# Moving most of a transpose stage, at the hand-over between two layers, into the turns of the loop before it

## The chip, the cores and the metric

The kernel runs on one core of a Trainium2 chip. The metric is the device time of one execution in microseconds (us); lower is better.

Engines are written as in the profile: PE is the matrix engine, PEld its weight loads, DVE is VectorE, ACT is ScalarE, POOL is GpSimd, SP issues DMAs. "L1211" is line 1211 of that kernel's source. The same statement has another line number in another kernel; a table below gives the ones that matter.

## The reference, cut to what matters

Four layers follow each other, A, B, A, B, each with a layer norm in front and a residual sum behind. `x` has 2048 tokens of width 640, in bf16.

```python
def _A_ref(x, w_r, w_i):                       # a 2D Fourier filter
    X = rfft2(x.astype(float32), axes=(-2, -1))
    X = X * (w_r + 1j * w_i)
    return irfft2(X, s=(S, D), axes=(-2, -1)).astype(bfloat16)

def _B_ref(x, mem0, Wq, Wk, Wv, Wo, seg_len):  # attention over 64 segments of 32 tokens
    mem = mem0
    for s in range(n_seg):
        h = concatenate([mem, x[:, s*seg_len:(s+1)*seg_len, :]], axis=1)
        # ... q, k, v, masked softmax, output projection o ...
        mem = o[:, :M, :].copy()
        outs.append(o[:, M:, :])

x = x + _A_ref(_layernorm(x), A_w_r, A_w_i)
x = x + _B_ref(_layernorm(x), B_mem0, B_Wq, B_Wk, B_Wv, B_Wo, B_seg_len)
x = x + _A_ref(...)                            # the same two layers once more
x = x + _B_ref(...)
```

The change touches the hand-over from A to B, which occurs twice (the prediction calls the two "layer 1" and "layer 2"). Layer A ends with an inverse DFT that yields `x` in 16 row tiles of 128 tokens. Layer B needs the normed `x` transposed (width on the partitions) in a buffer `hT`, and the sum of each segment, `u`, for a first guess of the memory.

## The kernel before: the parts that matter

The last stage of layer A. One turn computes one half transform (`psg`), evicts it on ACT, computes one row tile (`psy`), evicts it on ACT, and takes its statistics on DVE. Every second turn norms a pair of row tiles.

```python
def spectrum_d(s0):
    psg = pp.tile([128, 2, 512], FP32, name="psg", tag="pg", bufs=3)
    # ... six matmuls ...
    nc.scalar.copy(out=Gs[s0 % 3], in_=psg[:, :, 0:NF])

def tokens(s0):
    psy = pp.tile([128, 2, 512], FP32, name="psy", tag="pg", bufs=3)
    # ... six matmuls: residual, then the inverse transform of Gs ...
    nc.scalar.copy(out=halves(x[:, s0, :]), in_=psy[:, :, 0:320])
    _ln_stats(nc, st[q], mv[q], x[:, s0, :], t)        # DVE: bn_stats twice, bn_aggr

def norm(q):
    _ln_apply(nc, wk, mv[q], x[:, 2*q:2*q+2, :], xno, 2, g["eps"], on_dve=True)
    # ACT Ln and Exp, four DVE steps on 128x2, two DVE scalings of 128x640
    nc.sync.dma_start(out=xnd[:, 2*q:2*q+2, :], in_=xno)

for s0 in range(16 + 5):
    if s0 < 16:                                  spectrum_d(s0)
    if 1 <= s0 <= 16:                            tokens(s0 - 1)
    if s0 >= 2 and s0 % 2 == 1 and s0 < 18:      norm((s0 - 3) // 2)
    # ...
    if s0 >= 5:                                  handoff.add_u(pp, xna[:, s0-5, :], s0-5)
handoff.finish(pp)         # u, from the sums that add_u left in psu
pp.release()
handoff.transpose_all(xna)
```

`add_u` is five small matmuls per row tile, which add its segment sums to `psu`. After the loop come the transposes, 80 of 128x128, and their copies to `hT`, which DVE and ACT share:

```python
def transpose_all(self, xna):
    # a new PSUM pool `pt` with three buffers ...
    for c in range(5):
        ps = pt.tile([128, 16, 128], BF16, name="pstr", tag="pstr")
        for s0 in range(16):
            nc.tensor.transpose(out=ps[:, s0, :], in_=xna[:, s0, c*128:(c+1)*128], identity=ident[:])
        for g_ in range(4):
            # dst, src: 128 x 480
            (nc.vector.tensor_copy if g_ % 2 == 0 else nc.scalar.copy)(out=dst, in_=src)
        # ... four small copies for the last segments ...
```

Layer B then starts with 160 matmuls into `psvb`, which read `u` and not `hT`.

## Time and profile before

| | before |
|---|---|
| median of the runs at the start | 1658.21 us (3 runs, 1654.83 to 1659.44) |
| profiled span | 1658.3 us |
| PE busy | 94% of the span |
| first psg to first psvb, first and second hand-over | 49.9 us and 49.9 us |

The page of the profile gives these totals for the kernel before: busy time of each engine, and the engines' shares of the chain of work that ended last.

```profile
PE 1563.1 (94%) x14240; PEld 1081.0 (65%) x14241; DVE 790.0 (48%) x2300; ACT 835.6 (50%) x2528; POOL 282.4 (17%) x206
PE 41%; DVE 2%; DMA 2%; ACT 1%; issue 0%; SPq 0%; DVEq 0%; ACTq 0%
```

PE bounds the kernel as a whole. So only stretches in which PE is *not* busy can yield much, and the hand-over is one. The next lines are the windows view of the first hand-over, before. The columns are: stretch, its length, then busy time and count of PE, PEld, DVE, ACT and POOL, the granted PE clock (1.00 is full), the DMA share, GB/s. The stretches are the loop while PE has work, the rest of the loop, and the transpose stage.

```profile
94.00:122.70 28.70, 28.68 (x257) 20.57 (x256) 22.82 (x79) 23.27 (x43) 1.46 (x2) 1.00 0.91 321
122.70:130.00 7.30, 1.55 (x24) 1.18 (x25) 5.33 (x29) 2.12 (x7) 0.00 (x0) 0.76 0.97 307
130.00:143.90 13.90, 7.95 (x85) 7.59 (x83) 8.10 (x23) 6.54 (x20) 0.00 (x0) 0.75 0.28 77
```

PE is full for 28.7 us, and then busy for 9.5 of the 21.2 us that follow. PE's timeline shows what it waits for there. Its columns are start, duration, engine, line, operation, count, and in brackets the idle time before and what ended it.

```profile
94.00 1.83 PE L399 MATMUL psg<-A1gt_S,A1UT_S 128*128 128x321 bf16 x12 [0.91 <-DVE A1UT_S L350]
...
124.88 0.68 PE L1191 MATMUL psu<-sel,A1tok_S 128*128 128x64 bf16 x10 [2.20 <-DVE A1tok_S L120]
128.11 0.81 PE L1191 MATMUL psu<-sel,A1tok_S 128*128 128x64 bf16 x10 [2.55 <-DVE A1tok_S L120]
...
130.10 4.38 PE L1206 MATMUL pstr<-ident,A1tok_S 128*128 128x128 bf16 x48
136.98 3.47 PE L1206 MATMUL pstr<-ident,A1tok_S 128*128 128x128 bf16 x32 [2.49 <-DVE B1hT_S L1218]
143.94 6.20 PE L1248 MATMUL psvb<-u,B1wv_S 128*128 128x64 bf16 x160 [3.49 <-DVE B1hT_S L1218]
```

The last two psu groups wait for DVE's norm; the transposes and then psvb wait for the copies to `hT` (L1211 to L1218). One stretch of the timeline of all engines, before, shows how DVE and ACT share the copies of one pstr tile:

```profile
132.03 0.66 DVE L1211 COPY B1hT_S<-pstr 128x480 bf16<-128x480 bf16 x1 [1.49 <-PE pstr L1206]
132.77 0.56 ACT L1211 COPY B1hT_S<-pstr 128x480 bf16<-128x480 bf16 x1 [2.81 <-DVE B1hT_S L1211]
```

They do not work at the same time. ACT starts 0.08 us after DVE has ended, and what released it was DVE's copy, not the transposes. The waits view of the same window, before (who waited, for whom, us in total, times, longest), says so too:

```profile
ACT B1hT_S L1211 <- DVE B1hT_S L1211: 6.7, 5, 2.8
PE psvb L1248 <- DVE B1hT_S L1218: 3.5, 1, 3.5
```

The Trainium skill, "PSUM — Partial Sum Buffer", section "PSUM bank collisions raise a hardware error", gives a reason: the compiler's back end "adds a dependency between any two instructions on different engines that touch the same bank × 32-partition quadrant, reads and writes alike".

### The profile page before, as it was taken

To read this page: it belongs to the slowest core of one execution; us is meant where nothing else is said; L and a number is where in the kernel's file an instruction comes from. 1 tells how busy PE (TensorE), PEld (TensorE's weight loads), DVE (VectorE), ACT (ScalarE), POOL (GpSimd) and SP (SyncE) were. 2 spreads that over 40 slices of the span, in tenths; PEclk is the share of its full clock that TensorE was granted. 3 is DMA by queue.
4 is the path that set the end of the run, shared out by engine and by line. 5 is a ranking of instruction groups with operands and counts; after the bars stand their busy time and mean duration, and the time that the engine had idled before them with its cause. 6 is when DMAs were issued, how large, how long until landed. Compare 5 with 4: busy or idle time off the path is not lost. (4 is left out here: it accounts for less than half of the span.)

```text
span 1658.3 us, 36195 instructions
## 1 busy us (share of the span) xinstructions
PE 1563.1 (94%) x14240; PEld 1081.0 (65%) x14241; DVE 790.0 (48%) x2300; ACT 835.6 (50%) x2528; POOL 282.4 (17%) x206
## 2 busy tenths in 40 slices
PE   4887999999999999899988789999999999999998
PEld 2566666666666666677755666666666666666775
DVE  5772455555545554543356724545545454544110
ACT  5373566666666666511114636666666666663000
POOL 0810112121211111100026002121211111111000
PEclk9998999999999999999999899999999999999999
DMA  4472143434434343633302703434344343436241
GB/s 155 156 274 72 53 148 132 155 117 148 136 138 144 130 154 127 233 125 96 96 13 88 260 2 110 160 116 150 132 142 137 133 156 127 140 130 226 68 127 54
DMA packets 167873, 218.05 MB, mean 131 GB/s; under 512 B 7374, under 2 KB 141836, under 8 KB 159756
## 3 DMA queue, kind: packets, MB, share of 16 engines
q1 hardware_dynamic: 167084, 213.34, 38.5%
q8 instruction: 113, 1.85, 0.4%
q0 software_dynamic: 608, 2.30, 0.4%
q14 instruction: 68, 0.56, 0.1%
HBM read 170.52 MB, written 45.09 MB: 130 GB/s over the span
## 5 line engine op out<-in xcount | busy, mean ns | idle before, releaser
L846 PEld LDWEIGHTS <-bB_S 128*128 128x128 bf16 x3180 | 260.2, 97 | 185.9 <-issue 6.6
L990 DVE TENSOR_TENSOR bB_S<-pso,bB_S 128x480 bf16<-128x480 f32 (+1 forms) x320 | 189.4, 592 | 266.3 <-PE pso L981 249.4
L925 ACT ACTIVATE bB_S<-pss 128x269 bf16<-128x269 f32 (+5 forms) x576 | 213.3, 385 | 191.7 <-PE pss L922 177.2
L1140 PE MATMUL psx<-Wo_sb,bB_S 128*128 128x320 bf16 x2048 | 288.2, 299 | 3.9 <-DMA bB_S<-oTx_d 3.9
L1140 PEld LDWEIGHTS <-bB_S 128*128 128x128 bf16 x2048 | 197.2, 98 | 80.5 <-DMA bB_S<-oTx_d 4.6
L905 DVE CAST bB_S<-psk 128x495 bf16<-128x495 f32 (+3 forms) x320 | 191.3, 598 | 115.0 <-PE psk L846 84.8
L950 POOL TENSOR_TENSOR bB_S<-bB_S,bB_S 128x634 f32<-128x634 f32 x64 | 99.2, 1550 | 820.9 <-ACT bB_S L946 809.9
L926 DVE TENSOR_TENSOR bB_S<-bB_S,maskf 128x269 bf16<-128x269 bf16 (+5 forms) x576 | 162.9, 287 | 152.9 <-ACT bB_S L925 149.2
L914 ACT CAST bB_S<-psv 128x512 bf16<-128x512 f32 (+1 forms) x288 | 160.5, 557 | 83.8 <-PE psv L912 83.4
L890 ACT ACTIVATE bB_S<-psq 128x480 bf16<-128x480 f32 x300 | 152.5, 508 | 97.9 <-PE psq L846 97.9
L846 PE MATMUL psk<-B2hT_S,bB_S 128*128 128x495 bf16 (+3 forms) x800 | 165.0, 342 | 2.6 <-DVE bB_S L905 1.4
L846 PE MATMUL psk<-B1hT_S,bB_S 128*128 128x495 bf16 (+3 forms) x800 | 165.0, 342 | 1.7 <-DVE B1hT_S L1225 1.2
L912 PE MATMUL psv<-bB_S,B1hT_S 128*128 128x256 bf16 x1360 | 163.4, 272 | 0.2 <-DVE bB_S L905 0.2
L912 PE MATMUL psv<-bB_S,B2hT_S 128*128 128x256 bf16 x1360 | 163.4, 272 | 0.2 <-DVE bB_S L905 0.2
L922 PEld LDWEIGHTS <-bB_S 128*128 128x128 bf16 x1216 | 103.1, 98 | 90.1 <-issue 6.3
L846 PE MATMUL psq<-B2hT_S,bB_S 128*128 128x495 bf16 (+5 forms) x780 | 157.6, 336 | 0.1
L846 PE MATMUL psq<-B1hT_S,bB_S 128*128 128x495 bf16 (+5 forms) x780 | 157.5, 336 | 0.1
L922 PE MATMUL pss<-bB_S 128*128 128x132 bf16 (+8 forms) x1216 | 148.4, 216 | 3.0
L912 PEld LDWEIGHTS <-B1hT_S 128*128 128x128 bf16 x1360 | 128.7, 98 | 13.7 <-issue 0.3
L912 PEld LDWEIGHTS <-B2hT_S 128*128 128x128 bf16 x1360 | 128.6, 98 | 13.7 <-issue 0.3
L981 PE MATMUL pso<-bB_S,bB_S 128*128 128x132 bf16 (+8 forms) x1216 | 119.6, 216 | 0.0
L981 PEld LDWEIGHTS <-bB_S 128*128 128x128 bf16 x1216 | 91.2, 98 | 15.7 <-DVE oTmf L991 0.5
(225 smaller groups left out, 1555.1 us busy)
## 6 DMA issues: line engine op xcount, KB each, us to landing
bB_S<-Rd SPq DMA_DIRECT2D x62, 1059.5 KB
oTx_d<-bB_S SPq DMA_DIRECT2D x60, 512.0 KB
bB_S<-oTx_d SPq DMA_DIRECT2D x56, 512.0 KB
bB_S<-in_B_Wq_dram SPq DMA_DIRECT2D x32, 320.0 KB
bB_S<-in_B_Wk_dram SPq DMA_DIRECT2D x32, 320.0 KB
bB_S<-in_B_Wv_dram SPq DMA_DIRECT2D x32, 320.0 KB
bB_S<-oTx_d SPq DMA_DIRECT2D x14, 384.0 KB
Wo_sb<-in_B_Wo_dram SPq DMA_DIRECT2D x4, 1280.0 KB
```

Of the source, the lines that this page charges most:

```text
L846: nc.tensor.matmul(ps, lhsT=w[:, ch, hh * 128:(hh + 1) * 128], rhs=src[:, ch, lo:hi], start=(ch == 0), stop=(ch == 4))
L890: nc.scalar.mul(out=qv[:, :, 0:SEG], in_=x_view(ps, o, n)[:, :, 1:SW], mul=scale)
L905: nc.vector.tensor_copy(out=KTs[h % 2][:, lo:hi], in_=ps[:, 0:hi - lo])
L912: nc.tensor.matmul(ps[:, i * 256:(i + 1) * 256], lhsT=hT[:, ch, (t + i) * 128:(t + i + 1) * 128], rhs=w["Wv"][:, ch, :], start=(ch == 0), ...
L914: nc.scalar.copy(out=V[:, t:t + n, :].rearrange("p a b -> p (a b)"), in_=ps[:, 0:n * 256])
L922: nc.tensor.matmul(ps[:, off - o0:off - o0 + hi - lo], lhsT=KT[:, t * 128:(t + 1) * 128], rhs=QT[:, lo:hi], start=True, stop=True)
L925: nc.scalar.activation(out=E[:, 0:n], in_=ps[:, 0:n], func=ACTF.Exp)
L926: nc.vector.tensor_tensor(out=P[:, o0:o0 + n], in0=E[:, 0:n], in1=bs.mask[:, o0:o0 + n], op=ALU.mult)
L950: nc.gpsimd.tensor_tensor(out=accS, in0=accS, in1=sums_sb, op=ALU.add)
L981: nc.tensor.matmul(pso[:, lo - q0:hi - q0], lhsT=V[:, t, (h % 2) * 128:(h % 2 + 1) * 128], rhs=P[:, off:off + hi - lo], start=(i == 0), st ...
L990: nc.vector.tensor_tensor(out=oT.rearrange("p (r s j) -> p r s j", r=16, j=2)[:, :, s0:s0 + ns, :], in0=byclass(po), in1=rx, op=ALU.mult)
L1140: self.tc.nc.tensor.matmul(ps[:, 0:320], lhsT=lhs(h, k // 2), rhs=self.g["Wo_sb"][:, h, c0:c0 + 320], start=(h == 0), stop=(h == H - 1))
```

## The change

The intent is to hide the transposes under the DFT loop, where PE is at full clock, and to leave only those of the last four row tiles for the end. Within a turn the new order is: norm a pair whose statistics are complete; copy out the transposes that the turn before left in PSUM; start the next pair's norm; psg; psy; add_u for two rows; and last, four row tiles' transposes of two of the five column blocks. The small steps of the norm, on 128x2 elements, move from DVE to POOL. The five small transposes of the memory move into the loop too, to turn 4 (in the diff they are among what is left out), and `pstr` has one buffer in place of three.

```diff
-            for s0 in range(16 + 5):
-                if s0 < 16:
-                    spectrum_d(s0)
-                if 1 <= s0 <= 16:
-                    tokens(s0 - 1)
-                if s0 >= 2 and s0 % 2 == 1 and s0 < 18:
-                    norm((s0 - 3) // 2)
-                ...
-                    if s0 >= 5:
-                        handoff.add_u(pp, xna[:, s0 - 5, :], s0 - 5)
+            moved = None
+            for i in range(16 + 3):
+                if i >= 4 and i % 2 == 0:
+                    norm((i - 4) // 2)
+                if moved is not None:
+                    handoff.rows_out(*moved)
+                    moved = None
+                if i >= 3 and i % 2 == 1:
+                    inverse((i - 3) // 2)          # Ln, Exp on ACT, small steps on POOL
+                if i < 16:
+                    spectrum_d(i)
+                if 1 <= i <= 16:
+                    tokens(i - 1)
+                ...
+                if i >= 4 and i % 2 == 0:
+                    handoff.add_u(pp, xna[:, i - 4, :], i - 4)
+                    handoff.add_u(pp, xna[:, i - 3, :], i - 3)
+                if 6 <= i < 18 and (i - 6) % 4 < 3:
+                    moved = handoff.rows_in(pp, xna, (i - 6) // 4, (i - 6) % 4 * 2)
+            handoff.finish(pp)
+            moved = [handoff.rows_in(pp, xna, 3, 0, big=True), handoff.rows_in(pp, xna, 3, 4)]
+            for m in moved:
+                handoff.rows_out(*m)
         pp.release()
-            handoff.transpose_all(xna)
```

```diff
+    def rows_in(self, pp, xna, q, c0, big=False):       # transposes of four row tiles
+        # tile "pstr" (two column blocks), or "pstrb" (four) in a double bank of tag "pg"
+        for c in range(c0, c1):
+            for i in range(4):
+                nc.tensor.transpose(out=ps[:, c - c0, i, :], in_=xna[:, 4*q + i, c*128:(c+1)*128], ...)
+    def rows_out(self, ps, q, c0, c1):                   # their copies to hT
+        for c in range(c0, c1):
+            (nc.vector.tensor_copy if c % 2 == 0 else nc.scalar.copy)(   # 128 x 480
+                out=v[:, :, :, :, s0:s0 + 4], in_=...)
+        small = nc.scalar.copy if c0 == 4 else nc.vector.tensor_copy
+        small(...)                                        # 128 x 64 or less
+        # ... two more small ACT copies for the last four row tiles ...
```

So that one copy can serve four groups of segments, `hT` gets another layout: all columns from 512 on move up by `PRE`, and its length grows by 12.

```diff
+    def hcol(self, k):
+        return k + (self.PRE if k >= 512 else 0)
-        self.hT = self.ar.get("S2", f"{self.lname}hT").bf(5, self.st.NK)
+        self.hT = self.ar.get("S2", f"{self.lname}hT").bf(5, self.st.NK + 12)
```

| statement | line before | line after | e1, e7 | e4 |
|---|---|---|---|---|
| large copy to `hT` | L1211 | L1260 | L1269 | L1233 |
| last small copy to `hT` | L1218 | L1267 | L1276 | L1240 |
| transposes | L1206 | L1248 | L1257 | L1228 |
| add_u (psu) | L1191 | L1229 | L1238 | L1213 |
| psvb | L1248 | L1297 | L1306 | L1270 |

More of the change, by code (lines that the diff above doesn't have):

```diff
@@ L105, in _ln_stats, with _ln_inverse @@
     nc.vector.bn_aggr(out=mv[:, t, :], in_=st[:, t, :, :])
-def _ln_apply(nc, pool, mv, xin, xout, nt, eps_t, on_dve=False):
+def _ln_inverse(nc, pool, mv, nt, eps_t, small):
     rs = pool.tile([128, 4], FP32, name="lnrs", tag="lnrs")
@@ L113, in _ln_apply, with _ln_scale @@
     nc.scalar.activation(out=r0, in_=r0, func=ACTF.Exp, scale=-0.5)
-    nc.vector.scalar_tensor_tensor(out=t, in0=mv[:, :nt, 1], scalar=LN_EPS, in1=r0, op0=ALU.add, op1=ALU.mult)
-    nc.vector.tensor_tensor(out=t, in0=t, in1=r0, op=ALU.mult)
-    nc.vector.tensor_scalar(out=t, in0=t, scalar1=-0.5, scalar2=1.5, op0=ALU.mult, op1=ALU.add)
-    nc.vector.tensor_tensor(out=t, in0=t, in1=r0, op=ALU.mult)
+    if small is nc.vector:
+        small.scalar_tensor_tensor(out=t, in0=mv[:, :nt, 1], scalar=LN_EPS, in1=r0, op0=ALU.add, op1=ALU.mult)
+    else:
+        small.tensor_scalar_add(out=t, in0=mv[:, :nt, 1], scalar1=LN_EPS)
+        small.tensor_tensor(out=t, in0=t, in1=r0, op=ALU.mult)
+    small.tensor_tensor(out=t, in0=t, in1=r0, op=ALU.mult)
+    small.tensor_scalar(out=t, in0=t, scalar1=-0.5, scalar2=1.5, op0=ALU.mult, op1=ALU.add)
+    small.tensor_tensor(out=t, in0=t, in1=r0, op=ALU.mult)
+    return rs, nb
+def _ln_scale(nc, mv, rs, xin, xout, nt):
+    for t in range(nt):
+        nc.vector.tensor_scalar(out=xout[:, t, :], in0=xin[:, t, :], scalar1=mv[:, t, 0:1], scalar2=rs[:, t:t + 1], op0=ALU.subtract, op1=ALU.mult)
+def _ln_apply(nc, pool, mv, xin, xout, nt, eps_t, on_dve=False):
+    rs, nb = _ln_inverse(nc, pool, mv, nt, eps_t, nc.vector)
     if on_dve:
-        for t in range(nt):
-            nc.vector.tensor_scalar(out=xout[:, t, :], in0=xin[:, t, :], scalar1=mv[:, t, 0:1], scalar2=rs[:, t:t + 1], op0=ALU.subtract, op1=ALU.mult)
+        _ln_scale(nc, mv, rs, xin, xout, nt)
         return
@@ L128, in _ln_tiles @@
     st = pool.tile([128, 4, 2, nc.vector.BN_STATS_DIM], FP32, name="lnst", tag="lnst")
-    mv = pool.tile([128, 4, nc.vector.BN_AGGR_DIM], FP32, name="lnmv", tag="lnmv")
+    mv = pool.tile([128, 4, nc.vector.BN_AGGR_DIM], FP32, name="lnmv", tag="lnmv", bufs=3)
     return st, mv
-SLOT = dict(S1=20480, S2=10880, S3=12288, S4=10240, S5=12166, S6=11776)
+SLOT = dict(S1=20480, S2=10940, S3=12288, S4=10240, S5=12166, S6=11776)
 class _Cut:
@@ L417, in tokens, with inverse @@
                 nc.sync.dma_start(out=xd[:, 2 * q:2 * q + 2, :], in_=x[:, 2 * q:2 * q + 2, :])
+        rs = {}
+        def inverse(q):
+            rs[q], _ = _ln_inverse(nc, wk, mv[q], 2, g["eps"], nc.gpsimd if q < 7 else nc.vector)
         def norm(q):
             xno = xna[:, 2 * q:2 * q + 2, :]
-            _ln_apply(nc, wk, mv[q], x[:, 2 * q:2 * q + 2, :], xno, 2, g["eps"], on_dve=True)
+            _ln_scale(nc, mv[q], rs[q], x[:, 2 * q:2 * q + 2, :], xno, 2)
             nc.sync.dma_start(out=xnd[:, 2 * q:2 * q + 2, :], in_=xno)
@@ L424, in tokens @@
         with tc.manual_schedule(engines={nc.tensor.engine, nc.scalar.engine, nc.vector.engine}):
-            for s0 in range(16 + 5):
-                if s0 < 16:
-                    spectrum_d(s0)
-                if 1 <= s0 <= 16:
-                    tokens(s0 - 1)
-                if s0 >= 2 and s0 % 2 == 1 and s0 < 18:
-                    norm((s0 - 3) // 2)
-                if handoff is not None:
-                    if s0 < 10:
-                        handoff.wv_piece(s0)
-                    if s0 >= 5:
-                        handoff.add_u(pp, xna[:, s0 - 5, :], s0 - 5)
@@ L437, in tokens @@
-        if handoff is not None:
-            handoff.finish(pp)
+            moved = None
[11 more added lines that the diff above has]
+                    tokens(i - 1)
+                if handoff is None:
+                    continue
+                if i < 10:
+                    handoff.wv_piece(i)
+                if i == 4:
+                    handoff.memory(pp)
+                if i >= 4 and i % 2 == 0:
[3 more added lines that the diff above has]
+                    moved = handoff.rows_in(pp, xna, (i - 6) // 4, (i - 6) % 4 * 2)
@@ L439, in tokens @@
+            if handoff is not None:
+                handoff.finish(pp)
+                moved = [handoff.rows_in(pp, xna, 3, 0, big=True), handoff.rows_in(pp, xna, 3, 4)]
+                for m in moved:
+                    handoff.rows_out(*m)
         pp.release()
-        if handoff is not None:
-            handoff.transpose_all(xna)
 H, DH, MEM, SEG, NSEG = 32, 128, 8, 32, 64
@@ L526, in __init__ @@
             qpos[b:b + SW] = np.concatenate([MEM + np.arange(SEG), [MEM - 1]])
+        self.hgap = [(self.hcol(a), self.hcol(b)) for a, b in ((502, 512), (1007, 1024), (1519, 1536), (2035, 2048))]
         self.q0 = [0] + [self.qbase(g * GS) for g in range(1, self.NG)] + [self.NQ]
@@ L844, in chain @@
         def chain(w, hh, ps, src, lo, hi):
+            if src is hT:
+                lo, hi = st.hcol(lo), st.hcol(lo) + hi - lo
             for ch in range(5):
@@ L861, in q_x @@
                 n = GS if g_ < NG - 1 else 3
-                b = st.kbase(g_ * GS)
+                b = st.hcol(st.kbase(g_ * GS))
                 ps = pj.tile([128, 512], FP32, name="psq", tag="pj")
@@ L911, in v_tiles @@
                 for ch in range(5):
-                    nc.tensor.matmul(ps[:, i * 256:(i + 1) * 256], lhsT=hT[:, ch, (t + i) * 128:(t + i + 1) * 128], rhs=w["Wv"][:, ch, :],
+                    nc.tensor.matmul(ps[:, i * 256:(i + 1) * 256], lhsT=hT[:, ch, st.hcol((t + i) * 128):st.hcol((t + i) * 128) + 128], rhs=w["Wv"][:, ch, :],
                                      start=(ch == 0), stop=(ch == 4))
@@ L1171, in begin @@
     def begin(self):
-        self.hT = self.ar.get("S2", f"{self.lname}hT").bf(5, self.st.NK)
-        for a, b in ((502, 512), (1007, 1024), (1519, 1536), (2035, 2048)):
+        self.hT = self.ar.get("S2", f"{self.lname}hT").bf(5, self.st.NK + 12)
+        for a, b in self.st.hgap:
             self.tc.nc.gpsimd.memset(self.hT[:, :, a:b], 0.0)
@@ L1192, in add_u @@
                              skip_group_check=True)
-    def transpose_all(self, xna):
-        nc, g, st, hT, tc = self.tc.nc, self.g, self.st, self.hT, self.tc
-        ident, SW, GS = g["ident"], st.SW, st.GS
-        with tc.tile_pool(name="bs_pt", bufs=3, space=PSUM) as pt, tc.tile_pool(name="bs_pm", bufs=1, space=PSUM) as pm:
-            psm = pm.tile([128, 5, MEM], BF16, name="psm0")
-            for c in range(5):
-                nc.tensor.transpose(out=psm[:, c, :], in_=self.m0[:, c * 128:(c + 1) * 128], identity=ident[:MEM, :MEM])
-            nc.vector.tensor_copy(out=hT[:, :, 0:MEM], in_=psm[:])
-            nc.vector.tensor_copy(out=self.gq[:, :, 0:1], in_=psm[:, :, MEM - 1:MEM])
-            for c in range(5):
-                ps = pt.tile([128, 16, 128], BF16, name="pstr", tag="pstr")
-                for s0 in range(16):
-                    nc.tensor.transpose(out=ps[:, s0, :], in_=xna[:, s0, c * 128:(c + 1) * 128], identity=ident[:])
-                for g_ in range(4):
-                    b = st.kbase(g_ * GS)
-                    dst = hT[:, c, b:b + GS * SW].rearrange("p (w t) -> p w t", t=SW)[:, :, 1:SW].rearrange("p w (j s) -> p w j s", s=16)
-                    src = ps[:, :, 2 * GS * g_:2 * GS * (g_ + 1)].rearrange("p s (w j) -> p w j s", j=2)
-                    (nc.vector.tensor_copy if g_ % 2 == 0 else nc.scalar.copy)(out=dst, in_=src)
-                b = st.kbase(4 * GS)
-                dst = hT[:, c, b:b + 3 * SW].rearrange("p (w t) -> p w t", t=SW)[:, :, 1:SW].rearrange("p w (j s) -> p w j s", s=16)
-                nc.vector.tensor_copy(out=dst, in_=ps[:, :, 120:126].rearrange("p s (w j) -> p w j s", j=2))
-                b = st.kbase(NSEG - 1) + 1
-                nc.scalar.copy(out=hT[:, c, b:b + 16], in_=ps[:, :, 126])
-                nc.scalar.copy(out=hT[:, c, b + 16:b + SEG - st.TAIL], in_=ps[:, 0:16 - st.TAIL, 127])
-                nc.vector.tensor_copy(out=hT[:, c, st.TAILK:st.TAILK + st.TAIL], in_=ps[:, 16 - st.TAIL:16, 127])
@@ new lines, in memory @@
+    def memory(self, pp):
+        nc = self.tc.nc
+        psm = pp.tile([128, 5, 128], BF16, name="psm0", tag="pstr")
+        for c in range(5):
+            nc.tensor.transpose(out=psm[:, c, 0:MEM], in_=self.m0[:, c * 128:(c + 1) * 128], identity=self.g["ident"][:MEM, :MEM])
+        nc.vector.tensor_copy(out=self.hT[:, :, 0:MEM], in_=psm[:, :, 0:MEM])
+        nc.vector.tensor_copy(out=self.gq[:, :, 0:1], in_=psm[:, :, MEM - 1:MEM])
+    def rows_in(self, pp, xna, q, c0, big=False):
+        nc, c1 = self.tc.nc, min(5, c0 + (4 if big else 2))
+        if big:
+            ps = pp.tile([128, 4, 4, 128], BF16, name="pstrb", tag="pg", bufs=3)
+        else:
+            ps = pp.tile([128, 2, 4, 128], BF16, name="pstr", tag="pstr")
+        for c in range(c0, c1):
+            for i in range(4):
+                nc.tensor.transpose(out=ps[:, c - c0, i, :], in_=xna[:, 4 * q + i, c * 128:(c + 1) * 128], identity=self.g["ident"][:])
+        return ps, q, c0, c1
@@ new lines, in rows_out @@
+    def rows_out(self, ps, q, c0, c1):
+        nc, st, hT = self.tc.nc, self.st, self.hT
+        SW, GS, s0 = st.SW, st.GS, 4 * q
+        n = 4 if q < 3 else 3
+        b = st.hcol(st.kbase(4 * GS))
+        win = hT[:, :, b:b + 4 * SW].rearrange("p c (w t) -> p c w t", t=SW)
+        grp = hT[:, :, st.PRE:st.PRE + 4 * 512].rearrange("p c (g k) -> p c g k", g=4)[:, :, :, 0:GS * SW]
+        for c in range(c0, c1):
+            v = grp[:, c, :, :].rearrange("p g (w t) -> p g w t", t=SW)[:, :, :, 1:SW].rearrange("p g w (j s) -> p g w j s", s=16)
+            (nc.vector.tensor_copy if c % 2 == 0 else nc.scalar.copy)(
+                out=v[:, :, :, :, s0:s0 + 4], in_=ps[:, c - c0, :, 0:120].rearrange("p s (g w j) -> p g w j s", g=4, j=2))
+        small = nc.scalar.copy if c0 == 4 else nc.vector.tensor_copy
+        v = win[:, c0:c1, 0:n, 1:SW].rearrange("p c w (j s) -> p c w j s", s=16)
+        small(out=v[:, :, :, :, s0:s0 + 4], in_=ps[:, 0:c1 - c0, :, 120:120 + 2 * n].rearrange("p c s (w j) -> p c w j s", j=2))
+        if n == 3:
+            nc.scalar.copy(out=win[:, c0:c1, 3, 1 + s0:5 + s0], in_=ps[:, 0:c1 - c0, :, 126])
+            nc.scalar.copy(out=hT[:, c0:c1, st.hcol(st.TAILK):st.hcol(st.TAILK) + 4], in_=ps[:, 0:c1 - c0, :, 127])
@@ L1223, in scatter @@
             lo, hi = max(1, g_ * st.GS), min((g_ + 1) * st.GS, NSEG)
-            b = st.kbase(lo)
+            b = st.hcol(st.kbase(lo))
             nc.vector.tensor_copy(out=hT[:, :, b:b + (hi - lo - 1) * st.SW + 1:st.SW], in_=gq[:, :, lo:hi])
```

## The prediction

> **What bounds it now.** The page has PE busy 94% of 1658.3 us, and PE leads the chain of waits (41%). The exceptions are the two hand-overs from layer A to layer B. Take layer 1, in the timeline. The final stage's first matmul (psg) starts at 94.0; its 16 turns run at PE's pace, 1.80 us each, VectorE (DVE) almost full beside it (3.7 of 4 us), ScalarE (ACT) at 3.4 of 4. PE runs dry at 122.7. DVE works off its backlog to 128.4, then the 80 transposes and their 40 large evictions run alone. The first psvb matmul starts at 143.9: 49.9 us after psg. Layer 2 is the same (906.4 to 956.3). So some 21 us of poor PE work per layer could go, 43 us at most.
>
> **What the change removes and adds.** The 14 us transpose stage goes, save a quarter at the end. Into the loop come 60 of 80 transposes (an estimate of 0.06 us each, from N / 2.4 GHz plus 2.5 ns in the Trainium skill, "TensorE: Matmul & The Clock Gate", section "Wait — 56ns, not 53.3ns?"; the trace has only slower ones, 0.09 to 0.11 us, at a clock of 0.5 to 0.7): 0.3 us per turn on PE. DVE gets 9 evictions of 128x480 (0.65 us) and 6 small ones (0.2), ACT 6 of 0.56; DVE loses four small norm steps per pair (0.74 us), which go to GpSimd with a turn's slack. By busy time this fits in about 2.1 us a turn, and would save 8 to 10 us per layer.
>
> **What I think spoils it: waits in a ring.** In the built order, ACT's copy from a pstr tile waits for DVE's copy from the same tile, and DVE's small copy for ACT's. The present trace shows the same: ACT's first pstr copy starts 0.09 us after DVE's ends (132.77 after 132.68). The rows leave at the head of the turn, so ACT's psg and psy evictions stand behind DVE's copy, which stands behind the statistics of the turn before (1.05 us), which need ACT's psy eviction of that turn. One turn's ring: statistics 1.05, [norm 0.72 in even turns], DVE copy 0.65, ACT copy 0.56, [Ln and Exp 0.44 in odd turns], two casts 1.25, small latencies: about 4.2 us against PE's 2.1. Also the norm now comes after the preceding statistics and add_u waits for it in the same turn, so even turns without rows run at about 2.4 us.
>
> I laid the instructions of both orders end to end with these durations. For the kernel before this gives PE's last add_u at 34.6 us after psg (trace: 34.9) and DVE's end at 34.3 (34.4). For the kernel after: last psy about 50 us after psg, psvb at 56. So 6 us later than before, per layer; with slower copies or GpSimd up to 10. Were ACT not to wait for DVE, it would be 47: 2.7 us earlier.
>
> **Prediction.** Twice +6 us on 1658: 1669 us, 8 in 10 between 1648 and 1682. Faster by over 2%: 1%; within 2%: 95%; slower by over 2%: 4%. Shifted columns of hT should cost nothing: psy matmuls with odd starts (L411) take 301 ns, with even 298.
>
> **Right if:** psg to psvb is about 56 us in both layers; turns with rows last some 4 us; in the waits, ACT's hT copies wait for DVE's hT copies for several us, PE's psy and psg for ACT, add_u for the norm; the clock stays mostly at 1.00 in the loop; the rest of the program is unchanged. **Wrong if** ACT's copies overlap DVE's (psvb near 47), GpSimd's five steps take over 2.3 us (later still), or layer B's matmuls change speed.

## The result, and the profile after

| | before | after |
|---|---|---|
| median | 1657.38 us (4 runs) | 1682.70 us (4 runs, 1680.10 to 1684.68) |
| ratio | | 1.0153 (95%: 1.0131 to 1.0174) |
| results | correct | correct |

The ratio is the mean time of one kernel's fast runs over that of the other's of the same rounds, so it is not quite the ratio of the medians. The change costs 24 to 25 us. That is more than the 11 us predicted, and just above the top of the range, 1682.

The profiled spans can be cut at the first psg and the first psvb of each hand-over. The fourth column is a second look at the unchanged kernel after (run e5 below).

| stretch (us) | before | after | after again |
|---|---|---|---|
| start to first psg | 94.0 | 92.9 | 93.6 |
| first psg to first psvb, first hand-over | 49.9 | 62.3 | 60.7 |
| from there to the second first psg | 762.5 | 761.4 | 761.9 |
| first psg to first psvb, second hand-over | 49.9 | 60.7 | 60.7 |
| from there to the end | 701.9 | 705.6 | 704.0 |

So the loss lies where it was expected, in the two hand-overs, but each of them lost 10.8 us and more, not 6. The page after has PE's share of the span unchanged, at 94%:

```profile
PE 1574.9 (94%) x14240; PEld 1081.6 (64%) x14241; DVE 785.3 (47%) x2242; ACT 833.1 (50%) x2520; POOL 294.6 (18%) x276
```

The same number of matmuls takes 11.8 us more PE time, 9.7 us of it in the two hand-overs (38.2 us in each before, 43.8 and 42.3 after). The windows view after, at the first hand-over, shows a lower clock with it; the stretches are the loop to the last psy, the two turns behind it, and the end from the last psu to psvb. Columns as before.

```profile
92.90:140.70 47.80, 39.43 (x318) 25.98 (x317) 24.74 (x69) 26.46 (x52) 8.13 (x37) 0.89 0.57 200
140.70:148.20 7.50, 1.39 (x17) 0.76 (x15) 5.49 (x17) 1.89 (x5) 0.00 (x0) 0.70 0.76 234
148.20:155.20 7.00, 2.94 (x30) 2.70 (x31) 3.40 (x16) 2.56 (x9) 0.00 (x0) 0.50 0.57 173
```

In the loop no engine is full: PE is busy for 39.4, DVE for 24.7 and ACT for 26.5 of 47.8 us, where before PE was full and DVE and ACT were each busy for some 23 of 28.7. So there are waits to look for, and the timeline has them. And PE's clock has fallen, to 0.89 on average, and to 0.50 at the end.

One turn of the ring of waits, from the timeline of all engines after (from one psy eviction to the next):

```profile
112.29 0.69 ACT L427 CAST A1x_S<-psy 128x640 bf16<-128x640 f32 x1
...
113.02 0.89 DVE L104 BATCH_NORM_STATS2 lnst<-A1x_S 128x6 f32<-128x320 bf16 x2 [1.30 <-ACT A1x_S L427]
...
113.94 0.21 DVE L105 BATCH_NORM_AGGREGATE lnmv<-lnst 128x2 f32<-128x12 f32 x1
114.07 0.75 DVE L127 TENSOR_SCALAR A1tok_S<-A1x_S,lnmv,lnrs 128x640 bf16<-128x640 bf16 x2
...
114.73 0.73 DVE L1260 COPY B1hT_S<-pstr 128x480 bf16<-128x480 bf16 x1
...
115.50 0.76 ACT L1260 COPY B1hT_S<-pstr 128x480 bf16<-128x480 bf16 x1 [2.51 <-DVE B1hT_S L1260]
...
116.29 0.24 DVE L1264 COPY B1hT_S<-pstr 128x64 bf16<-128x64 bf16 x1 [0.83 <-ACT B1hT_S L1260]
116.59 0.37 PE L1248 MATMUL pstr<-ident,A1tok_S 128*128 128x128 bf16 x2 [1.39 <-DVE B1hT_S L1264]
...
116.69 0.71 ACT L427 CAST A1x_S<-psy 128x640 bf16<-128x640 f32 x1
```

Read it as a chain. DVE's statistics need ACT's psy eviction. The scaling and DVE's copy follow on DVE. ACT's copy from the same pstr tile waits 2.51 us for DVE's copy. DVE's small copy waits for ACT's. PE's next transposes wait for the small copy, as there is one pstr buffer. ACT's next psy eviction stands in ACT's queue behind its copy. From 112.29 to 116.69 this is 4.4 us for one row tile, where PE alone took 1.80 before.

The waits of that hand-over after confirm that this repeats:

```profile
ACT B1hT_S L1260 <- DVE B1hT_S L1260: 15.4, 8, 2.5
PE psu L1229 <- DVE A1tok_S L127: 8.5, 8, 3.4
ACT B1hT_S L1264 <- DVE B1hT_S L1260: 5.9, 4, 1.8
PE pstr L1248 <- DVE B1hT_S L1264: 5.1, 6, 1.4
PE psvb L1297 <- ACT B1hT_S L1267: 4.1, 1, 4.1
```

How far does such a wait reach? The last transposes go to the larger tile `pstrb`. In the built program (built from the same source) it fills banks 2 and 3: column blocks 0 and 1 lie in the one, 2 and 3 in the other. ACT's copy of block 1 and then DVE's copy of block 2 are these lines:

```profile
151.54 0.73 ACT L1260 COPY B1hT_S<-pstrb 128x480 bf16<-128x480 bf16 x1 [1.14 <-DVE B1hT_S L1260]
152.30 0.76 DVE L1260 COPY B1hT_S<-pstrb 128x480 bf16<-128x480 bf16 x1 [0.80 <-ACT B1hT_S L1260]
```

DVE waits for ACT here too, from one bank to the other, so a shared bank is not what this wait needs: the copies out of one tile are kept apart. The built program already holds this wait, before the compiler gets it. Copies to `hT` out of different tiles do overlap: ACT's from `pstrb` at 154.16 us runs during DVE's from `pstr`, 154.03 to 154.78.

The last of the waits listed is the one that answers to "PE psvb L1248" above. PE's timeline after, at the end of the stage, has it in its place:

```profile
142.17 0.68 PE L1229 MATMUL psu<-sel,A1tok_S 128*128 128x64 bf16 x10 [1.32 <-DVE A1tok_S L127]
144.24 0.58 PE L1248 MATMUL pstr<-ident,A1tok_S 128*128 128x128 bf16 x4 [1.39 <-DVE B1hT_S L1264]
148.19 0.81 PE L1229 MATMUL psu<-sel,A1tok_S 128*128 128x64 bf16 x10 [3.37 <-DVE A1tok_S L127]
148.81 1.89 PE L1248 MATMUL pstrb<-ident,A1tok_S 128*128 128x128 bf16 x16
150.50 0.63 PE L1248 MATMUL pstr<-ident,A1tok_S 128*128 128x128 bf16 x4
155.23 7.34 PE L1297 MATMUL psvb<-u,B1wv_S 128*128 128x64 bf16 x160 [4.10 <-ACT B1hT_S L1267]
```

The transposes end at 151.13, which is 58.2 us after psg (56.6 in the second hand-over, and 56.6 in both of the second look). The prediction had said 56. Then PE does nothing for 4.10 us until the last small copy of the last pstr tile has been made.

Two lines here can be held against the Trainium skill, "TensorE: Matmul & The Clock Gate". Its section "Wait — 56ns, not 53.3ns?" gives 55.6 ns for a warm and 106.7 ns for a cold matmul of 128 columns. The 16 cold transposes from 148.81 to 150.50 took 106 ns each, and eight warm ones in the loop (109.16 to 109.61) took 56 ns each: both agree. Its section "What's actually happening" says that the clock is halved after an idle window of some 3.4 us. The stretch with the idle times of 3.37 and 4.10 us has a granted clock of 0.50, and the psvb matmuls behind it lasted 241 ns in the median, where before it was 193. So far that agrees. But the half clock of this stretch began at 143.8, before the first of these idle times (144.8 to 148.2). It also came three times in the loop, for 3.4 us from 102.8, 116.5 and 130.1, where PE's longest idle time in the 7 us before was 1.39 us; in the 3.4 us before these spells PE was busy for 58, 48 and 52% of the time (the trace's clock records, set beside PE's busy time). So an idle window of 3.4 us was not needed for the half clock here.

### The profile page after: what moved, and what is told of

Its sections match the earlier page's. It is cut to its first block, busy times and chain, and to the rows that moved or that the text cites. A ratio compares the mean times of both kernels' runs of the same rounds, so it can differ in the third digit from the quotient of the medians.

```text
span 1682.9 us, 36213 instructions
## 1 busy us (share of the span) xinstructions
PE 1574.9 (94%) x14240; PEld 1081.6 (64%) x14241; DVE 785.3 (47%) x2242; ACT 833.1 (50%) x2520; POOL 294.6 (18%) x276
## 3 DMA queue, kind: packets, MB, share of 16 engines
q1 hardware_dynamic: 167084, 213.34, 38.2%
## 5 line engine op out<-in xcount | busy, mean ns | idle before, releaser
L960 PEld LDWEIGHTS <-bB_S 128*128 128x128 bf16 x1216 | 102.8, 97 | 90.5 <-issue 6.2
```

The source lines that it names most:

```text
L960: nc.tensor.matmul(ps[:, off - o0:off - o0 + hi - lo], lhsT=KT[:, t * 128:(t + 1) * 128], rhs=QT[:, lo:hi], start=True, stop=True)
```

## The experiments

After the result there were these theories for the 10.8 us per hand-over:

- **Ring**: DVE and ACT are kept apart on each pstr tile, and this chains the loop to 4.4 us a turn. Rival: it is the sheer amount of copies, or the norm's new place, whoever waits for whom.
- **Tail**: psvb waits for the last copy to `hT` because its PSUM pool is allocated after the old pool is released as a whole. Rival: it waits for `u`, or for the copies themselves, and would start no earlier with other pools.
- **Rest**: what remains is the new layout of `hT`, or the small steps on POOL.

All experiments were correct. They ran in batches on three chips, each batch beside runs of the kernel before on its chip; the ratios are to those runs. "Interval" is from the first psg to the first psvb, in the first and second hand-over; it is 49.9/49.9 before and 60.7/60.7 in the second look at after.

### e1: the double banks in pools of their own

The edit, against the kernel after. The three double banks of psg, psy and pstrb get one pool each; pstr and psu stay in `pp`. Every instruction keeps its engine and its place in the order.

```diff
+        pgs = [tc.alloc_tile_pool(name=f"{self.lname}_ps3{k}", bufs=1, space=PSUM) for k in range(3)]
         pp = tc.alloc_tile_pool(name=f"{self.lname}_ps3", bufs=1, space=PSUM)
+        def pg(shape, dt, name):
+            pg_n[0] += 1
+            return pgs[(pg_n[0] - 1) % 3].tile(shape, dt, name=name, tag="pg")
-            psg = pp.tile([128, 2, 512], FP32, name="psg", tag="pg", bufs=3)
+            psg = pg([128, 2, 512], FP32, "psg")
         # ... psy and pstrb likewise ...
         pp.release()
+        for p in reversed(pgs):
+            p.release()
```

> The changed kernel with each double bank of psg/psy in a PSUM pool of its own, apart from pstr and psu; nothing else moved. Theory (first psvb waits 4.1 us for the last pstr copy because the new pool's banks belong to a released pool that pstr was in): psvb starts at the end of the transposes, about 57.5 us after the first psg (changed kernel 62.3 and 60.7), the loop as before, total 8 us under the changed kernel, about 1674. Rival (psvb waits for hT or for ScalarE being late, whatever the pools): no change, about 1683.

Measured: 1668.53 us, ratio 1.0077 (1.0061 to 1.0094). Interval 56.4 and 56.3. PE's timeline of e1 at the end of the stage:

```profile
145.74 0.81 PE L1238 MATMUL psu<-sel,A1tok_S 128*128 128x64 bf16 x10 [3.57 <-DVE A1tok_S L127]
146.36 1.89 PE L1257 MATMUL pstrb<-ident,A1tok_S 128*128 128x128 bf16 x16
148.05 0.63 PE L1257 MATMUL pstr<-ident,A1tok_S 128*128 128x128 bf16 x4
148.47 2.20 PE L1306 MATMUL psvb<-u,B1wv_S 128*128 128x64 bf16 x61
```

psvb follows the last transpose with no idle time (the view ends after 61 of its 160 matmuls). In the built program of the kernel after, the first psvb tile lies in bank 0, pstr in bank 6 and pstrb in banks 2 and 3, so the wait of 4.10 us guarded no data of that tile: it came from releasing one pool that held them all. The tail theory is shown, its rival is out. The change gains 4.3 us per hand-over, and psvb itself ran faster, 4.9 and 6.0 us where the second look at after had 7.2 and 7.2. In the first hand-over of e1 the half clock, which had begun at 142.2 us, ended at 149.0, half a us into psvb; in the second look it lasted to 160.0, almost to psvb's end. About half of the loss of 24 us is this.

### e2: ACT takes its block of the pair first

```diff
-        for c in range(c0, c1):
+        for c in sorted(range(c0, c1), key=lambda c: c % 2 == 0):
```

Now ACT's copy of a pstr tile comes first in program order, and DVE's waits for ACT's, with the same copies on the same engines.

> The changed kernel with one swap: of the two columns of a pstr tile ScalarE's is issued first and VectorE's waits for it. Theory of the ring (ScalarE's casts stand behind VectorE's copy and so behind the statistics): ScalarE's waits for VectorE's hT copy shrink from 15 us per layer to the c=4 ones alone (6 us), turns with rows shrink by about 1 us, first psg to psvb about 55 us, total about 15 us under the changed kernel, 1668. Rival (VectorE, ScalarE and PE simply have too much work in the loop, or the statistics and norm alone set the pace): no change, 1683, since no work is taken away.

Measured: 1662.62 us, ratio 1.0041 (1.0024 to 1.0058). Interval 52.7 and 52.7. The waits of e2 in the hand-over:

```profile
ACT B1hT_S L1264 <- DVE B1hT_S L1260: 6.9, 4, 2.7
DVE B1hT_S L1260 <- ACT B1hT_S L1260: 4.5, 4, 2.6
```

The wait of 15.4 us of ACT for DVE is gone from the list, DVE waits 4.5 us for ACT in its place, and the last psy comes 40.3 us after psg instead of 46.0. So the direction of that wait alone, with no work added or removed, was worth 8 us per hand-over. The ring theory is shown as a main part of the loss. psvb still waited 3.8 us at the end.

### e3: the copies of the new path on DVE

```diff
-            (nc.vector.tensor_copy if c % 2 == 0 else nc.scalar.copy)(
+            nc.vector.tensor_copy(
-        small = nc.scalar.copy if c0 == 4 else nc.vector.tensor_copy
+        small = nc.vector.tensor_copy
```

> The changed kernel with all large and small pstr copies of the loop on VectorE, none on ScalarE. Ring theory: although VectorE gets 6 more copies of 0.7 us, ScalarE's casts no longer wait for it, psg to psvb about 55 us, total about 1669. Rival (VectorE's load is the limit): VectorE has 4 us more work in the loop per layer, so 4 us per layer slower than the changed kernel, about 1691.

Measured: 1664.84 us, ratio 1.0048 (1.0029 to 1.0066). Interval 53.6 and 53.0, last psy 40.7. The two small ACT copies at the end of each of the last two tiles stay on ACT. DVE does *more* here than in the kernel after, and the hand-over is some 7 us shorter. Hence DVE's load is not what bounds the kernel after. What this edit takes away is the alternation of two engines on one tile.

### e4: the new order of the norm, without the transposes

The kernel before, with the new order of `norm`, `inverse` and `add_u` and the POOL steps, but with all transposes in one stage at the end and the old `hT`.

```diff
+            for i in range(16 + 3):
+                if i >= 4 and i % 2 == 0:
+                    norm((i - 4) // 2)
+                if i >= 3 and i % 2 == 1:
+                    inverse((i - 3) // 2)
+                # ... spectrum_d, tokens, as after ...
+                if i >= 4 and i % 2 == 0:
+                    handoff.add_u(pp, xna[:, i - 4, :], i - 4)
+                    handoff.add_u(pp, xna[:, i - 3, :], i - 3)
         pp.release()
         if handoff is not None:
             handoff.transpose_all(xna)        # as before
```

> The kernel before with only the turn order of the change (norm first in the next turn, Ln and Exp first on ScalarE, add_u for two rows in that turn, small norm steps on GpSimd); all 80 transposes stay in one stage at the end. Theory (the norm placed one turn earlier takes the slack away: add_u waits for the norm, Ln for the statistics): last add_u about 41 us after psg instead of 34.9, psg to psvb about 56.5, total 14 us over the kernel before, about 1671. Rival (only the row copies cost): as the kernel before or a little faster, 1655 to 1659.

Measured: 1666.05 us, ratio 1.0061 (1.0044 to 1.0077). Interval 56.4 and 56.4; last psy 35.8 and 35.7 (before: 28.2). Its waits in the hand-over:

```profile
ACT lnnb L112 <- DVE lnmv L105: 11.9, 8, 2.1
...
PE psu L1213 <- DVE A1tok_S L127: 8.3, 8, 2.6
```

The new order of the norm alone costs 6.5 us per hand-over, before any transpose moves. ACT's Ln now stands at the head of the turn, in front of ACT's evictions, and waits for the statistics of the turn just ended; add_u waits for a norm of the same turn. In the kernel before, both had a turn or two between them.

### e5: the kernel after once more

No edit. It was run to see whether the half-clock spells inside the first hand-over's loop belong to the kernel or to that one execution.

> The changed kernel itself once more, to have it beside the kernel before and the others on one chip. Expected 1.5% over the kernel before (1680); the four parts measured so far say the same thing only if it does not come near 1668. The layers' first psg to psvb near 61, with half-clock spells in some turns.

Measured: 1682.15 us, ratio 1.0144 (1.0119 to 1.0168). Interval 60.7 and 60.7. The result repeats. The first hand-over was 1.6 us shorter than in the first profile, so that much of 62.3 belongs to the one execution, and 10.8 us is the sound figure per hand-over.

### e6: one more turn between the norm's steps

Against after: the scaling comes at the odd turn `i-5`, Ln and Exp behind the evictions of the turn, add_u two turns later, and the transposes two turns later.

```diff
-            for i in range(16 + 3):
-                if i >= 4 and i % 2 == 0:
-                    norm((i - 4) // 2)
+            for i in range(16 + 5):
+                if i >= 5 and i % 2 == 1:
+                    norm((i - 5) // 2)
-                if i >= 3 and i % 2 == 1:
-                    inverse((i - 3) // 2)
                 # ... spectrum_d, tokens ...
+                if i >= 3 and i % 2 == 1 and i < 18:
+                    inverse((i - 3) // 2)
-                if i >= 4 and i % 2 == 0:                      # add_u rows i-4, i-3
+                if i >= 6 and i % 2 == 0:                      # add_u rows i-6, i-5
-                if 6 <= i < 18 and (i - 6) % 4 < 3:
+                if 8 <= i < 20 and (i - 8) % 4 < 3:
```

> The changed kernel with norm one turn later, Ln and Exp behind the casts of their turn, add_u and the row transposes two turns later; the copies and their order on the engines unchanged. Theory: this gives back the slack of norm and add_u (e4 showed 7 us per layer for it alone), but the ring through ScalarE's copy remains, and the loop is two turns longer: psg to psvb about 57, 9 us in all under the changed kernel. If the ring were nothing but the norm's place, it would come near 50.

Measured: 1669.81 us, ratio 1.0076 (1.0058 to 1.0094). Interval 56.9 and 57.0; last psy 41.9 and 41.7. The slack gains 3.7 us per hand-over. ACT still waits 14.2 us for DVE's copies, so the ring survives it.

### e7: slack, another split of the copies, and separate pools

Against e6: ACT takes column blocks 0, 1 and 3, DVE only 2 and 4, ACT first within each tile, all small copies of that kind on DVE; and the pools of e1.

```diff
-        for c in range(c0, c1):
+        for c in sorted(range(c0, c1), key=lambda c: c % 3 == 2 or c == 4):
-            (nc.vector.tensor_copy if c % 2 == 0 else nc.scalar.copy)(
+            (nc.vector.tensor_copy if c in (2, 4) else nc.scalar.copy)(
-        small = nc.scalar.copy if c0 == 4 else nc.vector.tensor_copy
+        small = nc.vector.tensor_copy
         # and the pools of e1
```

> e6 together with ScalarE's copies first (ScalarE takes columns 0, 1 and 3, VectorE columns 2 and 4 and the small copies, waiting for ScalarE and not the reverse) and with the pools of e1. Theory: no wait of ScalarE for VectorE is left in the loop, PE waits little, psvb does not wait for the last copies: psg to psvb about 41 to 43 against 49.9 of the kernel before, total 14 to 18 us under the kernel before, about 1639. Rival (the loop is full: VectorE and ScalarE can't take the copies beside the casts and statistics): psg to psvb 48 or more, no faster than the kernel before.

Measured: **1639.12 us, ratio 0.9893 (0.9876 to 0.9910)**. Interval 41.4 and 41.8; last psy 32.0. It is faster than both kernels, by about 17 us against before. The windows of e7 in the first hand-over (the loop to the last psy, and the rest to psvb) and the end of PE's timeline:

```profile
92.60:124.70 32.10, 31.34 (x292) 22.72 (x292) 22.35 (x64) 26.39 (x49) 7.54 (x33) 1.00 0.81 287
124.70:134.00 9.30, 5.23 (x72) 4.71 (x71) 7.07 (x32) 4.38 (x12) 0.89 (x5) 0.78 0.90 280
```

```profile
133.61 0.64 PE L1257 MATMUL pstr<-ident,A1tok_S 128*128 128x128 bf16 x4
134.04 2.18 PE L1306 MATMUL psvb<-u,B1wv_S 128*128 128x64 bf16 x37
```

PE is busy for 31.3 of 32.1 us at a clock of 1.00 with the transposes in the loop: the intent of the change holds once the waits are out of the way. The next question was which part gave how much (e8, e10, e11).

### e8: e7 with the small steps on DVE

```diff
-            rs[q], _ = _ln_inverse(nc, wk, mv[q], 2, g["eps"], nc.gpsimd if q < 7 else nc.vector)
+            rs[q], _ = _ln_inverse(nc, wk, mv[q], 2, g["eps"], nc.vector)
```

> e7 with the small norm steps on VectorE for every pair, as in the kernel before. Theory: VectorE is then the fullest engine of the loop (0.74 us per pair more), psg to psvb 2 us later per layer than e7, total 4 us over e7. If GpSimd's steps (five of 0.2 us and gaps) were a burden, it would be faster than e7.

Measured: 1641.37 us, ratio 0.9904 (0.9886 to 0.9923). Interval 42.9 and 43.1, 1.5 and 1.2 us longer than in e7 in the one profile of each. In the total times the intervals of the two overlap, so whether POOL helps here is not settled. It is a small matter in any case.

### e9: the kernel before with only the small steps on POOL

```diff
-            _ln_apply(nc, wk, mv[q], x[:, 2 * q:2 * q + 2, :], xno, 2, g["eps"], on_dve=True)
+            rs, _ = _ln_inverse(nc, wk, mv[q], 2, g["eps"], nc.gpsimd if q < 7 else nc.vector)
+            _ln_scale(nc, mv[q], rs, x[:, 2 * q:2 * q + 2, :], xno, 2)
```

> The kernel before with nothing but the small norm steps moved to GpSimd, in the kernel's own turn order. Theory: harmless but no gain, since PE sets the pace of that loop and GpSimd's five steps (1.35 us) take longer than VectorE's four (0.74 us) in the chain of the last norms: last add_u 0 to 1.4 us later per layer, total 0 to +3 us, about 1658. Rival (the GpSimd steps are what made e4 slow): 7 us per layer later, about 1670.

Measured: 1657.40 us, ratio 1.0001 (0.9983 to 1.0019). Interval 50.7 and 49.5. This part of the change does nothing by itself, for good or ill. The five steps last 0.19 to 0.22 us each on POOL.

### e10: slack and ACT first

e6 with the one-line edit of e2.

```diff
-        for c in range(c0, c1):
+        for c in sorted(range(c0, c1), key=lambda c: c % 2 == 0):
```

> e6 with ScalarE's copy first in each tile, as in e2, columns still shared as in the change (VectorE 0, 2, 4), one pool. From the parts: e2 gave 8 us per layer, e6 4; if both remove different waits they nearly add: psg to psvb about 50 to 51, total near the kernel before, about 1657 to 1660. If they remove the same wait, it stays at 53 and 1662.

Measured: 1662.67 us, ratio 1.0036 (1.0019 to 1.0054). Interval 51.0 and 50.6; last psy 37.3 and 37.0. The loop gains from both, by 3 us over e2. The total does not: it is that of e2 (1.0041), within the intervals. Part of the loop's gain is given back behind it: from the last psy to psvb it takes 13.6 us, where e2 took 12.4, and psvb ran at half clock, for 7.3 and 7.1 us, where e2 had 6.2 and 6.2. That is read from one profile of each kernel.

### e11: e7 without the separate pools

```diff
-        pgs = [...]          # e7 with the one pool of the kernel after
```

> e7 with one PSUM pool, as in the change. Theory: psvb waits for the last copies, 4 us later per layer than e7: psg to psvb about 46, total 8 us over e7, about 1647, still under the kernel before.

Measured: 1648.31 us, ratio 0.9953 (0.9936 to 0.9969). Interval 46.0 and 45.7; last psy 32.0 as in e7. So the other split of the copies, with the small ones on DVE, over e10, is worth 5 us per hand-over, and the pools on top of it another 4.6 and 3.9 us: psvb waits 3.96 us here and not at all in e7. e7 and e11 together repeat e1 on a second kernel.

### e12: the kernel before with only the new layout of `hT`

```diff
+    def hcol(self, k):
+        return k + (self.PRE if k >= 512 else 0)
-        self.hT = self.ar.get("S2", f"{self.lname}hT").bf(5, self.st.NK)
+        self.hT = self.ar.get("S2", f"{self.lname}hT").bf(5, self.st.NK + 12)
         # and st.hcol(...) around each column index of hT
```

> The kernel before with nothing but the changed column layout of hT (7 columns of gap before the second group, so that layer B's matmuls read from odd columns). The kernels with rows in the loop spent 0 to 4 us more in the second layer B in their profiles than the three with the old layout. If the layout costs: 2 to 4 us over the kernel before, with the second layer's 32 heads taking 505 to 508 us instead of 504. As I predicted (it costs nothing): within 1 us of the kernel before.

Measured, with five rounds: 1658.38 us, ratio 1.0019 (1.0005 to 1.0033), so about 3 us, with an interval from 0.8 to 5.5. Interval 49.6 and 49.9, as before. The tile view of the matmuls that read `hT` into psk, before and in e12 (durations are minimum, median, maximum in ns):

```profile
L846 PE MATMUL psk<-B1hT_S,bB_S x800: 217/372/375, 166.3 to 670.6; 128*128 128x495 bf16 x64, 128*128 128x502 bf16 x32, 128*128 128x499 bf16 x32, 128*128 128x128 bf16 x32
```

```profile
L852 PE MATMUL psk<-B1hT_S,bB_S x800: 217/373/376, 165.7 to 670.4; 128*128 128x495 bf16 x64, 128*128 128x502 bf16 x32, 128*128 128x499 bf16 x32, 128*128 128x128 bf16 x32
```

They last 1 ns longer, 373 for 372. That repeats: PE's busy time on psk was 331.1 us and on psq 334.2 us or more (both stream `hT`) in all eleven profiles with the new layout, and 330.0 and 333.4 us in all three with the old one (before, e4, e9). psv, which has `hT` as its weights, took 326.8 or 326.9 in all fourteen. So 1.9 us of the cost lie in the matmuls that stream `hT` from the new columns. The rest is not placed: the psx matmuls, which do not read `hT`, took 289.3 us in e12 for 288.2 before, but 288.2 in eight other profiles with the new layout too, and in this one profile the stretch between the hand-overs was 3.6 us shorter than before and the last one 3.4 us longer. Why the new columns take longer is left open.

### The parts side by side

| kernel | ratio to before | interval, first / second | last psy after psg | psvb waits for a copy |
|---|---|---|---|---|
| before | 1 | 49.9 / 49.9 | 28.2 | 3.5 us |
| after (second look) | 1.0144 | 60.7 / 60.7 | 46.0 | 4.1 us |
| e1, pools | 1.0077 | 56.4 / 56.3 | 46.0 | no |
| e2, ACT first | 1.0041 | 52.7 / 52.7 | 40.3 | 3.8 us |
| e6, slack | 1.0076 | 56.9 / 57.0 | 41.9 | 4.1 us |
| e10, slack and ACT first | 1.0036 | 51.0 / 50.6 | 37.3 | 4.0 us |
| e11, slack and other split | 0.9953 | 46.0 / 45.7 | 32.0 | 4.0 us |
| e7, e11 and pools | 0.9893 | 41.4 / 41.8 | 32.0 | no |
| e4, new norm order alone | 1.0061 | 56.4 / 56.4 | 35.8 | 3.5 us |

## Why the prediction was right or wrong

The direction and the main mechanism were right, the size was not: 1669 us were predicted and 1682.7 measured, beyond the range.

1. **"ACT's copy from a pstr tile waits for DVE's copy from the same tile, and DVE's small copy for ACT's": right.** The waits after show 15.4 us of the first, and the timeline shows the whole ring. e2 turns that wait round and gains 8 us per hand-over. But the way from the ring to PE was another than predicted. "PE's psy and psg for ACT" did not come: psg never waited for ACT, and psy once, for 0.6 us. PE stood at the next transposes, 5.1 us for the one pstr buffer to be emptied, and at add_u (point 3). Whether a second pstr buffer would have freed PE was not tested.
2. **"Turns with rows last some 4 us": right.** The turn shown above lasted 4.4 us, the one after it 3.6 (from 116.69 to 120.29).
3. **"add_u waits for it in the same turn": right.** 8.5 us of "PE psu" for "DVE A1tok_S" after. e4 shows that this and the new place of Ln cost 6.5 us by themselves.
4. **"Last psy about 50 us after psg, psvb at 56. So 6 us later than before, per layer": this is the step that failed, and its last term above all.** 56 was a good figure for the end of the transposes, which came at 56.6 us in three of the four hand-overs profiled. Psvb was taken to start there, since it reads `u` and not `hT`. It started 4.1 us later, at 60.7, because its pool could not be had until the last reader of the old pool was done. e1 takes that wait away and psvb starts at 56.4. This term was sized at 0 and measured 4.1 us per hand-over, with over 1 us more in psvb itself in three of the four hand-overs, where its matmuls then ran mostly at half clock. The split within the 56 was off as well: the last psy came at 46.0 (47.7 in the first profile) and not at 50, and the end of the loop took that much longer. The two errors cancelled, so 56 was partly luck.
5. **Durations of the copies: too small.** The prediction took 0.65 us for DVE and 0.56 for ACT, from the trace before. In the new pattern a copy of the same 128x480 elements took 0.71 and 0.76. A turn of the ring contains one of each, so it is 0.26 us longer for this.
6. **"The clock stays mostly at 1.00 in the loop": wrong.** It was 0.89 in the loop of the first profile, 0.93 in the second. The lower clock of the first profile goes with the 1.6 us that its first hand-over took longer.
7. **"Shifted columns of hT should cost nothing": wrong, by a small amount.** e12 measures 0.19%, about 3 us, of which 1.9 lie in psk and psq. The prediction had reasoned from psy matmuls of 301 and 298 ns.
8. **"GpSimd's five steps take over 2.3 us" as a danger: did not come.** From the start of the first to the end of the last it was 1.66 us (99.20 to 100.86), and e9 finds no effect on the time.
9. **"The rest of the program is unchanged": nearly.** Outside the hand-overs the second look is 1.1 us longer than the kernel before (-0.4, -0.6 and +2.1). That is less than single profiles differ by: the last stretch of the same kernel is 705.6 in one and 704.0 in the other.

The sum of the second look: two hand-overs at +10.75 and +1.1 elsewhere give 22.6 us, which is the difference of the two profiled spans (1680.9 and 1658.3). The sum predicted was twice 6. The missing part is twice 4.8, of which 4.1 is the wait of psvb. The rest, 0.7 us per hand-over, agrees with transposes that ended at 56.6 and not at 56.

Where did the expected gain go? It was there to be had: e7 shows the transposes under the loop at 32.0 us for the last psy, against 28.2 without them, with PE full at a clock of 1.00, and a hand-over 8 us shorter than before. The kernel as changed turned it into waits: of ACT for DVE on the shared tile, of ACT and PE for a norm placed too close, and of psvb for a pool. The first two do not quite add: singly they give 8 (e2) and 3.7 us (e6) per hand-over, both together 9.7 and 10.1 (e10), and with the other split of the copies 15 (e11).

## What to carry to other kernels

When work is moved under a loop of another engine, count the waits that the new instructions bring, not only their busy time: two engines that empty one PSUM tile took turns here, even across its banks, so give the whole tile, or the first part of it, to the engine whose queue holds the next critical eviction. Leave a full turn between a result and its reader in each engine's order. And look at what the first matmul of the next stage waited for in the profile before: if it is something that it doesn't read, the pools are released too coarsely, and the wait will stay with the last copy wherever that is moved.

## What the Trainium skill lacked or had wrong

- "PSUM — Partial Sum Buffer", section "PSUM bank collisions raise a hardware error": no page among those read says that the copies of one tile can be kept apart even where they read different banks. In the kernel after, DVE's copy from bank 3 waited 0.80 us for ACT's copy of the same tile from bank 2, by a wait in the program as built.
- "TensorE: Matmul & The Clock Gate", section "What's actually happening": the half clock came here without the idle window of some 3.4 us that its table names, with PE busy for 48% of the 3.4 us before the spell at 116.5 us and never idle for more than 1.39 us.
- No page among those read says that the first tile of a new PSUM pool can wait for the last reader of a pool released before, even in another bank. That is a matter of the framework and not of the chip, but it belongs beside that section too, which explains waits by bank: here psvb in bank 0 waited 4.10 us for a copy from bank 6, and e1 removed that wait.
- "SBUF — State Buffer", section "Operand start alignment", speaks of which starts are legal and says that its runs timed nothing. e12 gives a first figure for shifted column starts of matmul operands: 0.19% of the kernel (0.05% to 0.33%), with psk matmuls of 373 for 372 ns in every profile. Whether the starts are the cause stayed open.
- "GPSIMD Engine Reference", section "Elementwise — side-by-side cycle accounting", compares VectorE and GpSimd at N = 2048, where GpSimd takes 1.96 times as long. For a tensor_tensor on 128x2 the traces have 196 ns on GpSimd and 160 ns on VectorE, 1.2 times.
